# Four small elementwise steps of a gated-attention and GEGLU kernel moved from VectorE to GpSimd

## The chip, the cores and the metric

The kernel runs on one core of a Trainium2 chip. The metric is device time in microseconds (us). Most executions of a kernel agree within some tenths of a per cent. On one core, a run counts as slow when it is over 1.5% above the fastest of the same kernel.

The profile's engines are PE (TensorE, matmuls), PEld (TensorE weight loads), DVE (VectorE), ACT (ScalarE), POOL (GpSimd) and SP (SyncE). L189 means line 189 of the kernel that is being profiled. Kernels with inserted lines have shifted numbers.

## The reference, cut to what matters

The lines of the second part are condensed.

```python
# attention part: q, k, v, a_re, a_im are (4, 8, 768, 48), float32
mag = np.sqrt(a_re * a_re + a_im * a_im)
scale = np.minimum(mag, 0.999) / (mag + 1e-06)           # the clamp
a_re_n, a_im_n = (a_re * scale, a_im * scale)
for t in range(S):                                       # a recurrence over the sequence
    new_re = ar * S_re - ai * S_im
    new_im = ar * S_im + ai * S_re
    kv = np.einsum('bhd,bhe->bhde', k[:, :, t], v[:, :, t])
    S_re, S_im = (new_re + kv, new_im)
    y[:, :, t] = np.einsum('bhd,bhde->bhe', q[:, :, t], S_re)
# ... x = y as (3072, 384) tokens ...
ffn_out = gelu(x @ w_gate) * (x @ w_val) @ w_out         # d_ff = 1536
res_gate = 1.0 / (1.0 + np.exp(-(x @ w_res)))
return x + res_gate * ffn_out                            # the residual add
```

The kernel replaces the recurrence by cumulative sums of log-magnitude and phase over blocks of the sequence. Each of the 12 groups holds 256 positions. The sums are carried from group to group.

## The kernel before

The four steps that move are marked.

```python
    def p1_steps(g):                       # log-magnitude of group g
        ...
        def s3():
            act(out=T["s", g], in_=T["s", g], func=AF.Ln, bias=1.0)
            lm = T["lm", g]
            nc.vector.scalar_tensor_tensor(out=lm, in0=T["s", g], scalar=0.5, in1=lm, op0=OP.mult, op1=OP.add)  # L188
            nc.vector.tensor_scalar(out=lm, in0=lm, scalar1=LNMAX, scalar2=None, op0=OP.min)                    # L189: clamp

    def carry(g):                          # phase carried from the group before
        ...
            nc.vector.tensor_tensor(out=P, in0=T["th", g - 1][:, DM:W], in1=T["th", g][:, 0:DM], op=OP.add)     # L215
            if s > 1:
                nc.vector.tensor_tensor(out=P, in0=P, in1=T["P", g - 1], op=OP.add)                             # L217

    def cs_t(g, c):                        # phase -> fraction of a turn
        ...                                # matmuls L227, L229 (L229 reads P), then L234, L235 on DVE
        if c == C - 1:
            nc.vector.scalar_tensor_tensor(out=fg[:, :, 0, :], in0=fg[:, :, 1, :], ...)                         # L237

    def turn(nm, g, srcs):                 # a row, turned to partitions by way of DRAM
        ...
        for i, src in enumerate(srcs):
            nc.gpsimd.dma_start(out=md[i:i + 1, :], in_=src)                                                    # L253
        for u in range(2):
            nc.gpsimd.dma_start(out=m[u * D:(u + 1) * D]..., in_=md...)                                         # L256: two halves

    def decay3(g):                         # M: the decay of the carried state
        m = T["m2", g]
        M = mp.tile([128, H], FP, tag="M", name="M")
        nc.vector.tensor_tensor(out=M[0:DD], in0=m[0:DD, 0], in1=m[0:DD, 1], op=OP.mult)                        # L273
        nc.vector.tensor_tensor(out=M[0:DD], in0=M[0:DD], in1=T["m1", g][0:DD, 0], op=OP.mult)                  # L274
    ...
    def op_step(u, jj):                    # output projection; ot comes from a pool of two buffers
        ...
        nc.vector.scalar_tensor_tensor(out=ot, in0=T["sg", u][:, jj], scalar=1.0, in1=ps, ...)                  # L437
        nc.vector.tensor_tensor(out=ot, in0=ot, in1=T["x", u * 4 + jj], op=OP.add)                              # L438: residual add
        nc.sync.dma_start(out=out[t0:t0 + 128, :], in_=ot)
```

GpSimd issues the turn transfers, the weight loads and the loads of `v`. M (L273) needs both halves of a turn transfer, and it stands in DVE's program order among the `fg` and `xT` work: in this kernel behind the second `fg` and `xT` of X1 and X2 (M of `m_1264` at 139.79 us, of `m_1910` at 186.16 us).

ScalarE's table loads cut the time into stretches. Pro is the prologue. Y0 to Y4 are the stretches with the gelu table, where the gate and value matmuls run. X1 to X4 are the stretches between them (Ln, Exp, Arctan, Sin). A tail follows.

## Time and profile before

The kernel before took 343.4 us (median of 3 runs, 342.9 to 344.4). The profiled execution spans 341.4 us.

| stretch | length, us | TensorE busy, us | granted clock |
|---|---|---|---|
| Pro (prologue) | 94.0 | 40.6 | 0.75 |
| Y0 | 26.0 | 24.4 | 1.00 |
| X1, Y1 | 20.8, 26.4 | 17.3, 25.7 | 1.00, 1.00 |
| X2, Y2 | 20.1, 26.6 | 16.1, 26.1 | 1.00, 1.00 |
| X3, Y3 | 20.7, 25.6 | 16.2, 25.3 | 1.00, 1.00 |
| X4, Y4 | 18.5, 26.0 | 17.3, 25.7 | 1.00, 1.00 |
| tail | 36.9 | 32.8 | 1.00 |

In the Y stretches the TensorE has hardly any idle time. In the X stretches it has about 13 us in all. So a lighter DVE can only help in X. A rule for reading what follows: work slides across the border of an X and the Y behind it, so such a pair is read as one number.

These are lines of the page of the kernel before: the span; busy time, share of the span and instruction count of four engines; and the activity in 40 equal slices, in tenths (PEclk is the granted TensorE clock).

```profile
span 341.4 us, 5552 instructions
PE 267.3 (78%) x2054; PEld 160.6 (47%) x2080; DVE 245.4 (72%) x440; ACT 203.0 (59%) x338; POOL 67.1 (20%) x104
...
PE   0330544298689979899897999779999989999995
DVE  1322696249999649999389998499994799855443
POOL 9423710050522224102232000150001300000000
PEclk9996585559699999999999999999999999999999
```

DVE is busy 72% of the time and GpSimd 20%, which is what invites the change.

These are the groups of DVE instructions by line and shape. After the bar come the total busy us and the mean ns of one, then the idle time before them.

```profile
L330 DVE TENSOR_TENSOR atm<-at,mask_81 128x512 bf16<-128x512 f32 x48 | 32.8, 683 | 7.2 <-PE at L327 7.2
...
L438 DVE TENSOR_TENSOR ot<-ot,x 128x384 f32<-128x384 f32 x24 | 13.2, 552 | 0.3
...
L237 DVE SCALAR_TENSOR_TENSOR fg<-fg 128x768 f32<-128x768 f32 x12 | 11.4, 949 | 0.0
...
L285 DVE TENSOR_TENSOR kE<-k,Ei 128x768 bf16<-128x768 f32 x12 | 11.4, 947 | 0.0
...
L189 DVE TENSOR_SCALAR ar<-ar 128x768 f32<-128x768 f32 x12 | 6.9, 592 | 0.1
```

The moved steps cost DVE 0.59 us (clamp) and 0.55 us (each add).

This is one line of GpSimd's timeline in X2: start, duration, then the instruction. Both halves of the transfer that M needs are issued back to back.

```profile
177.82 1.51 POOL L256 DMA_DIRECT2D m_1910<-dm_1907  x2 [0.63 <-issue]
```

### The profile page before, as it was taken

Reading aid. Unit: us, or ns where it says so; the run is one execution under the profiler, and the core shown is the slowest. Engines: PE = TensorE matmul, PEld = TensorE weight load, DVE = VectorE, ACT = ScalarE, POOL = GpSimd, SP = SyncE. Lnnn points to the kernel's source line nnn. Section 1 sums busy time; section 2 is a strip of 40 time slices with the busy share of each in tenths; the row PEclk is TensorE's granted clock in tenths of the full one; section 3 lists DMA queues with packets and bytes.
Section 4 is the critical chain, followed back from the end, with each engine's and each line's share of the span. In section 5 each row is a group of like instructions: output and inputs, shape, how many; then the busy total and the mean of one; then the engine's idle time right before and its main releaser. Section 6 shows DMA issues by size and latency. Waiting matters only on the chain.

```text
span 341.4 us, 5552 instructions
## 1 busy us (share of the span) xinstructions
PE 267.3 (78%) x2054; PEld 160.6 (47%) x2080; DVE 245.4 (72%) x440; ACT 203.0 (59%) x338; POOL 67.1 (20%) x104
## 2 busy tenths in 40 slices
PE   0330544298689979899897999779999989999995
PEld 0110224275256545465554566445665556565452
DVE  1322696249999649999389998499994799855443
ACT  3365434349665696756896656977568275662530
POOL 9423710050522224102232000150001300000000
PEclk9996585559699999999999999999999999999999
DMA  9999999999999999527422620021000210002002
GB/s 139 136 139 175 176 184 196 175 170 171 155 167 162 169 133 172 109 46 72 25 63 54 118 46 2 2 48 47 3 2 1 50 46 2 0 2 92 2 1 92
DMA packets 135258, 30.25 MB, mean 89 GB/s; under 512 B 127168, under 2 KB 135232, under 8 KB 135232
## 3 DMA queue, kind: packets, MB, share of 16 engines
q1 hardware_dynamic: 103296, 23.60, 40.6%
q0 software_dynamic: 31936, 6.31, 21.9%
q8 instruction: 16, 0.26, 0.3%
q14 instruction: 10, 0.08, 0.1%
HBM read 31.33 MB, written 4.76 MB: 106 GB/s over the span
## 4 chain that ended last, share of the span: by engine, by line
PE 47%; DMA 18%; DVE 15%; ACT 9%; issue 7%; POOL 3%; ACTq 0%; DVEq 0%; POOLq 0%
PE vp L414 12%; PE gp L410 11%; PE op L434 6%; DMA dm_266<-ar 4%; DMA v<-in_v_dram 4%; PE tp L320 3%; PE at L327 3%; PE tp L317 3%; PE rp L426 3%; DMA dm_663<-Ei 2%; ACT L445 2%; DVE fg L237 2%; DVE r L234 2%; DMA dm_219<-ar 2%; ACT CS L119 2%
## 5 line engine op out<-in xcount | busy, mean ns | idle before, releaser
L410 PE MATMUL gp<-xT,wg 128*128 128x512 bf16 x196 | 61.5, 382 | 7.6 <-DVE xT L401 4.6
L414 PE MATMUL vp<-xT,wv 128*128 128x512 bf16 x210 | 60.3, 382 | 0.3
L322 ACT COPY qk<-tp 96x512 bf16<-96x512 bf16 x48 | 27.9, 581 | 28.3 <-PE tp L320 15.1
L180 DVE TENSOR_TENSOR ai<-s,ai 128x768 f32<-128x768 f32 x12 | 11.1, 955 | 38.5 <-ACT s L119 26.9
L330 DVE TENSOR_TENSOR atm<-at,mask_81 128x512 bf16<-128x512 f32 x48 | 32.8, 683 | 7.2 <-PE at L327 7.2
L410 PEld LDWEIGHTS <-wg 128*128 128x128 bf16 x216 | 20.0, 98 | 23.0 <-issue 8.9
L317 PE MATMUL tp<-ident,Q 128*96 128x128 bf16 x192 | 20.1, 231 | 13.4 <-DVE qk L323 8.6
L142 POOL DMA_DIRECT2D v<-in_v_dram x24 | 21.3, 902 | 43.0 <-PE y L367 22.4
L414 PEld LDWEIGHTS <-wv 128*128 128x128 bf16 x216 | 20.4, 98 | 19.3 <-issue 0.8
L317 PEld LDWEIGHTS <-Q 128*96 128x96 bf16 x192 | 17.3, 131 | 21.4 <-issue 10.0
L323 DVE COPY qk<-tp 96x512 bf16<-96x512 bf16 x48 | 19.9, 414 | 10.1 <-ACT qk L322 9.6
L203 PE MATMUL csl<-ar,lt0a 128*128 128x384 f32 x24 | 12.3, 601 | 18.6 <-DVE ar L189 18.5
L119 ACT ACTIVATE CS<-fg,hpi 128x768 bf16<-128x768 f32 x12 | 11.2, 935 | 24.1 <-DVE fg L237 24.1
L445 ACT ACT_TABLE_LOAD x18 | 23.1, 1283 | 1.0 <-PEq L547 0.7
L320 PE MATMUL tp<-ident,K 128*96 128x128 bf16 x192 | 22.1, 235 | 0.0
L227 PE MATMUL cst<-ai,lt0b 128*128 128x384 f32 x24 | 11.6, 568 | 13.4 <-ACT ai L119 13.1
L327 PE MATMUL at<-qk 96*128 96x128 bf16 x192 | 20.4, 228 | 0.1
L437 DVE SCALAR_TENSOR_TENSOR ot<-sg,op 128x384 f32<-128x384 f32 x24 | 13.2, 549 | 9.4 <-PE op L434 9.4
L365 PE MATMUL y<-v,atm 128*128 128x48 bf16 x192 | 17.9, 187 | 2.5 <-DVE atm L330 2.4
L365 PEld LDWEIGHTS <-atm 128*128 128x128 bf16 x192 | 13.5, 98 | 12.8 <-DVE atm L330 11.6
L320 PEld LDWEIGHTS <-K 128*96 128x96 bf16 x192 | 17.3, 133 | 0.0
L357 PEld LDWEIGHTS <-K 128*96 128x96 bf16 x160 | 13.3, 138 | 6.5 <-DVE K L292 4.2
(155 smaller groups left out, 626.3 us busy)
## 6 DMA issues: line engine op xcount, KB each, us to landing
ar<-in_a_re_dram SPq DMA_DIRECT2D x24, 192.0 KB, 5.7
ai<-in_a_im_dram SPq DMA_DIRECT2D x24, 192.0 KB, 5.5
q<-in_q_dram SPq DMA_DIRECT2D x24, 192.0 KB, 5.1
k<-in_k_dram SPq DMA_DIRECT2D x24, 192.0 KB, 5.0
out_dram<-ot SPq DMA_DIRECT2D x24, 192.0 KB, 1.9
v<-in_v_dram POOLq DMA_DIRECT2D x24, 96.0 KB, 6.3
wg<-in_moe_w_gate_dram POOLq DMA_DIRECT2D x4, 288.0 KB, 9.2
wv<-in_moe_w_val_dram POOLq DMA_DIRECT2D x4, 288.0 KB, 10.5
```

The lines of the kernel that those rows point to most:

```text
L142: nc.gpsimd.dma_start(out=t[:, c], in_=rows(v, g, c))
L317: nc.tensor.transpose(out=tp[0:DD, j * 128:j * 128 + 128], in_=Q(x), identity=ident)
L320: nc.tensor.transpose(out=tp[0:DD, 512 + j * 128:640 + j * 128], in_=K(x), identity=ident)
L322: nc.scalar.copy(out=qk[0:DD, 0:512], in_=tp[0:DD, 0:512])
L323: nc.vector.tensor_copy(out=qk[0:DD, 512:1024], in_=tp[0:DD, 512:1024])
L327: nc.tensor.matmul(out=at[:, j], lhsT=qk[0:DD, 512 + j * 128:640 + j * 128], rhs=qk[0:DD, j * 128:j * 128 + 128], start=True, stop=True)
L330: nc.vector.tensor_tensor(out=atm, in0=at, in1=mask4, op=OP.mult)
L365: nc.tensor.matmul(out=ys, lhsT=st["atm", hg][:, j], rhs=V(h), start=True, stop=first)
L410: nc.tensor.matmul(out=gp, lhsT=wg[:, fi, ffi * 128:(ffi + 1) * 128], rhs=xT[:, fi, :], start=(fi == 0), stop=(fi == KD - 1))
L414: nc.tensor.matmul(out=vp, lhsT=wv[:, fi, ffi * 128:(ffi + 1) * 128], rhs=xT[:, fi, :], start=(fi == 0), stop=(fi == KD - 1))
L434: nc.tensor.matmul(out=ps, lhsT=h2[:, ffi, jj * 128:(jj + 1) * 128], rhs=wo[:, ffi, :], start=(ffi == 0), stop=(ffi == KF - 1))
L445: tab(nc.scalar.preload_act_table_set(nm))
```

## The change

The intent is to unload DVE by giving four steps to the engine that is idle most of the time. Here is the whole diff, with lines of context cut.

```diff
@@ p1_steps, s3
-            nc.vector.tensor_scalar(out=lm, in0=lm, scalar1=LNMAX, scalar2=None, op0=OP.min)
+            nc.gpsimd.tensor_scalar(out=lm, in0=lm, scalar1=LNMAX, scalar2=None, op0=OP.min)
@@ carry
-            nc.vector.tensor_tensor(out=P, in0=T["th", g - 1][:, DM:W], in1=T["th", g][:, 0:DM], op=OP.add)
+            nc.gpsimd.tensor_tensor(out=P, in0=T["th", g - 1][:, DM:W], in1=T["th", g][:, 0:DM], op=OP.add)
             if s > 1:
-                nc.vector.tensor_tensor(out=P, in0=P, in1=T["P", g - 1], op=OP.add)
+                nc.gpsimd.tensor_tensor(out=P, in0=P, in1=T["P", g - 1], op=OP.add)
@@ op_step
-        nc.vector.tensor_tensor(out=ot, in0=ot, in1=T["x", u * 4 + jj], op=OP.add)
+        nc.gpsimd.tensor_tensor(out=ot, in0=ot, in1=T["x", u * 4 + jj], op=OP.add)
```

The diff doesn't show that the scheduler of this framework places the instructions anew, so the order on every engine changes as well. One such move matters: in X1 and X2, M now stands ahead of the second `fg`.

## The prediction

> **What bounds the kernel now.** Three regimes (activity by slices, busy time by windows).
> (1) Up to about 90 us the TensorE is mostly idle. The DMA engines are full (tenths at 9), and the chain of waits runs through small GpSimd-issued turn transfers: 21.8 us dm_219 (6.9 us), 31.3 m_247 (5.6), 44.8 dm_266 (13.9, behind the weight loads in the same queue).
> (2) From 96 us on, phases that run gate/value matmuls are TensorE-bound (23.2 of 24, 24.3 of 25, 25.6 of 26 us busy).
> (3) Between them are phases of about 20 us (120-142, 167-189, 214-233) with TensorE at 18.5 of 22, 17.8 of 22, 14.7 of 19 us. Their chain is ScalarE Ln/Exp, then an unbroken DVE row up to the second fg (L237), then Sin, table load, Gelu. Only here can a lighter DVE pay; 12 us of TensorE idle is the ceiling.
>
> **What moves (groups by line).** DVE loses 12 clamps (0.59 us each), 8+4 carry adds (0.55), 24 residual adds (0.55): 26.5 of 245 us. DVE instructions follow each other about 0.47 us apart, so a middle phase loses two clamps and three residual adds ahead of the second fg: about 2.3 us. GpSimd gains 48 instructions. Estimate, from the Trainium skill, "GPSIMD Engine Reference", section "Performance versus the Vector engine" (about 2.6 cycles per element with two inputs, 1.8 with one): 0.9-1.2 us each, so GpSimd busy rises from 67 to about 115 us. The trace before has no such instruction to check it.
>
> **Critical path.** Clamp and carry are used a phase later, except in the prologue; the residual add only feeds the output, except the last one. By themselves they are off the path. What matters is GpSimd's in-order queue, which also issues the turn DMAs. The instruction order of the changed kernel puts
> - the clamp of group 2 ahead of all weight loads. It waits for L188 (38.0 us before), so weights start about 3.5 us later, and dm_266 lands behind them;
> - clamps and residual adds between the two halves of m_1264 and m_1910. M (L273) stands on DVE ahead of the second fg in those phases, so DVE will wait for their landing: I estimate 3-4 us each (the last half issued at about 136 and 182 us, 3-4 us to land), more than the 2.3 us saved. In the phase at 214-233 us m_2538 is ahead of the residual adds: there the gain of about 2 us stays.
> Also, DVE operations with two SBUF inputs (L180, L188, L237, L280, L285, L292) may block against GpSimd's reads (Trainium skill, "SBUF — State Buffer", section "Who interferes with whom"). The trace before doesn't show it; I allow 0.2-0.4 us per GpSimd instruction, which returns about half of the 26 us.
> Sum: prologue 0 to +3 (the DVE row at 81-95 us loses 1.2), phase 120-142 +2, 167-189 +1, 214-233 -1.5, 259-280 +0.5, tail +0.7 (a slower residual add plus a hop).
>
> **Prediction.** 346.0 us, 8 in 10 between 339.5 and 353.0. Faster by over 2%: 0.04; within 2%: 0.76; slower by over 2%: 0.20.
>
> **Signs.** Right: DVE busy about 222-232 us; GpSimd 105-125; weights issued from about 40 us; DVE waits of some us at M for m_1264 and m_1910; two-input DVE operations with longer means; the last phases' TensorE busy time unchanged. Wrong: no waits at M and gelu starting earlier in every middle phase (then 338-340 us); or GpSimd instructions of 2 us and more (then over 350).
>
> **What would make it wrong.** The whole order was rescheduled: more attention work precedes the stall near 55-64 us, which may hide the later weights. Delayed v loads may let the first a-tiles land sooner. Port blocking may be far heavier than allowed.

## More of the kernel before

L237 and L285 read two operands from SBUF. L330 reads one from SBUF and one from PSUM.

## The result, and the profile after

The changed kernel is correct and slower. It took 356.64 us (median of 4 runs, 354.1 to 360.6; the longest counts as slow, and the three fast ones, up to 357.0, have the median 356.33), and the kernel before took 343.73 us in the same rounds. The ratio is 1.035, 95% interval 1.029 to 1.042. Ratios in this document are the mean time of one kernel's fast runs over that of the other's in the same rounds, so they are not quite the ratio of the medians that stand beside them. The profiled run is a fast one.

The same lines of the page of the changed kernel:

```profile
span 354.6 us, 5635 instructions
PE 274.0 (77%) x2080; PEld 160.7 (45%) x2080; DVE 232.0 (65%) x392; ACT 203.6 (57%) x338; POOL 139.4 (39%) x152
...
PE   0330507795399987799884999898999989999994
DVE  1312666677887477898395997398984699853431
POOL 6673490534942159502159400079500720003013
PEclk9995656588889999899999899999999999999998
```

DVE fell by 13.4 us only. GpSimd gained 72 us, where about 48 were expected. TensorE became busier by 6.7 us with the same matmuls. A few matmul records are missing in the first trace (x2054 against x2080), which may be part of that; the clock row shows another reason: it now dips in several slices.

Groups by line and shape of the changed kernel, DVE then GpSimd:

```profile
L330 DVE TENSOR_TENSOR atm<-at,mask_81 128x512 bf16<-128x512 f32 x48 | 32.9, 686 | 13.6 <-PE at L327 13.6
...
L237 DVE SCALAR_TENSOR_TENSOR fg<-fg 128x768 f32<-128x768 f32 x12 | 13.5, 1125 | 0.1
...
L285 DVE TENSOR_TENSOR kE<-k,Ei 128x768 bf16<-128x768 f32 x12 | 12.8, 1070 | 0.0
```

```profile
L438 POOL TENSOR_TENSOR ot<-ot,x 128x384 f32<-128x384 f32 x24 | 27.6, 1157 | 60.6 <-DVE ot L437 59.5
...
L189 POOL TENSOR_SCALAR ar<-ar 128x768 f32<-128x768 f32 x12 | 28.1, 2344 | 15.4 <-DVE ar L188 15.2
```

A clamp takes 2.34 us on GpSimd (at best 2.12) where DVE took 0.59. An add takes 1.16 us (at best 0.90) where DVE took 0.55. DVE's operations with two SBUF inputs became longer (L237 from 949 to 1125 ns). L330, with one input in PSUM, did not (683 and 686). Over all DVE groups that both kernels have, the lengthening adds up to 7.9 us (the sum over groups of the difference of means times the count).

GpSimd's timeline of the changed kernel in X2. The clamp now stands between the two halves of the transfer:

```profile
183.70 2.12 POOL L189 TENSOR_SCALAR ar<-ar 128x768 f32<-128x768 f32 x1 [0.84 <-DVE ar L188]
185.81 0.91 POOL L438 TENSOR_TENSOR ot<-ot,x 128x384 f32<-128x384 f32 x1
186.67 0.83 POOL L256 DMA_DIRECT2D m_1910<-dm_1907  x1
187.54 2.83 POOL L189 TENSOR_SCALAR ar<-ar 128x768 f32<-128x768 f32 x1
190.34 0.79 POOL L256 DMA_DIRECT2D m_1910<-dm_1907  x1
```

DVE's timeline of the changed kernel at the same place. The bracket is the idle time before an instruction, and what ended it:

```profile
188.31 0.54 DVE L234 TENSOR_SCALAR r<-cst 128x384 f32<-128x384 f32 x1
193.10 0.66 DVE L273 TENSOR_TENSOR M<-m_1910 96x8 f32<-96x8 f32 x1 [4.25 <-DMA m_1910<-dm_1907]
```

DVE does nothing for 4.25 us, in front of the second `fg`, `xT` and Q. In X1 it waits 2.25 us for `m_1264` in the same way. Two things meet here: the transfer is later, and M stands ahead of the second `fg` (which runs at 194.62 us) and no longer behind it.

On the TensorE this becomes a gap, as the waits of TensorE before and after show (what it waited for: us in total, times, longest). The 2.1 us of the kernel before lie in the prologue; ahead of Y1 and Y2 it waited 0.97 and 0.78 us there:

```profile
PE gp L410 <- DVE xT L401: 4.6, 4, 2.1
```

```profile
PE gp L410 <- DVE xT L401: 10.1, 4, 4.9
```

The gap costs more than its own length. The next fence has the changed kernel at the end of X1, by stretches of 1 us. The columns are the length, then busy us (and count) of PE, PEld, DVE, ACT and POOL, then the granted clock, the DMA share and GB/s.

```profile
141.00:142.00 1.00, 0.00 (x0) 0.00 (x0) 1.00 (x2) 0.00 (x0) 0.67 (x1) 1.00 1.32 185
142.00:143.00 1.00, 0.00 (x0) 0.00 (x0) 1.00 (x3) 0.00 (x0) 0.00 (x0) 1.00 1.44 200
143.00:144.00 1.00, 0.18 (x1) 0.10 (x1) 1.00 (x5) 0.46 (x1) 0.00 (x0) 1.00 0.48 58
144.00:145.00 1.00, 1.00 (x5) 0.37 (x4) 1.00 (x2) 1.00 (x2) 0.84 (x2) 0.69 0.02 2
145.00:146.00 1.00, 1.00 (x7) 0.75 (x6) 1.00 (x4) 0.98 (x2) 0.99 (x2) 0.50 0.13 1
146.00:147.00 1.00, 1.00 (x4) 0.30 (x2) 1.00 (x2) 0.99 (x2) 1.00 (x1) 0.50 0.18 18
147.00:148.00 1.00, 1.00 (x4) 0.40 (x3) 1.00 (x2) 0.34 (x2) 1.00 (x1) 0.60 0.00 0
```

After 3.42 us without a matmul the clock is granted at half for about 3.4 us. Over these four stretches that takes 0.31 + 0.50 + 0.50 + 0.40 = 1.7 us of full-speed matmul time. The Trainium skill, "TensorE: Matmul & The Clock Gate", section "Part 1: The HAM clock gate", states this behaviour: an idle window of about 3.4 us sets the array to half rate, and about as long a busy window releases it. Gaps of 3.42 and 4.9 us are each followed by 0.50 for about 3.4 us. But no length of gap is shown above which the clock falls. A gap of 2.50 us in X2/Y2 of e4 (below) left it at 1.00, while in e6 it fell to 0.50 at 239.67 us with no gap of over 1.33 us in the stretch before. That stretch of e6, in the same columns, shows TensorE busy for 1.44 of 3.41 us:

```profile
236.26:239.67 3.41, 1.44 (x18) 0.95 (x19) 3.41 (x4) 1.46 (x2) 3.33 (x5) 1.00 0.02 2
```

Lengths of the pairs in the profiled executions, with some of the experiments that follow:

| kernel | Pro+Y0 | X1+Y1 | X2+Y2 | X3+Y3 | X4+Y4 | tail | span |
|---|---|---|---|---|---|---|---|
| before | 120.0 | 47.2 | 46.7 | 46.2 | 44.5 | 36.9 | 341.4 |
| after | 121.8 | 51.0 | 52.1 | 47.3 | 44.6 | 37.9 | 354.6 |
| e6: after, M moved | 120.8 | 47.9 | 47.0 | 50.5 | 44.3 | 37.6 | 348.0 |
| e7: before, M moved | 119.4 | 46.9 | 46.5 | 46.3 | 43.2 | 36.9 | 339.1 |
| e10: e7, residual add on GpSimd | 118.2 | 49.3 | 48.3 | 49.2 | 44.3 | 38.0 | 347.3 |
| e13: e7, GpSimd repeats all four | 118.1 | 52.6 | 50.8 | 51.6 | 44.4 | 38.3 | 355.7 |
| e14: e7, GpSimd only writes | 117.1 | 53.5 | 48.2 | 48.6 | 43.2 | 38.3 | 348.9 |
| e15: e7 again | 116.5 | 46.9 | 46.5 | 46.2 | 43.2 | 36.9 | 336.2 |

Pro+Y0 differs by 2.9 us between e7 and e15, which are the same kernel, while all their other pairs agree within 0.1 us. So differences of less than 3 us in the first column are not read. Of the change's 13.2 us, 3.9 + 5.4 = 9.3 us are in the pairs 1 and 2, the two in which DVE waits at M.

### The profile page after: what moved, and what is told of

Read it like the earlier page. It is cut to its first block, busy times and chain, and to the rows that moved or that the text cites. A ratio compares the mean times of both kernels' runs of the same rounds, so it can differ in the third digit from the quotient of the medians.

```text
span 354.6 us, 5635 instructions
## 1 busy us (share of the span) xinstructions
PE 274.0 (77%) x2080; PEld 160.7 (45%) x2080; DVE 232.0 (65%) x392; ACT 203.6 (57%) x338; POOL 139.4 (39%) x152
## 4 chain that ended last, share of the span: by engine, by line
PE 52%; SPq 15%; DMA 10%; DVE 8%; ACT 6%; issue 4%; POOL 4%; POOLq 0%; ACTq 0%; DVEq 0%
PE gp L410 13%; PE vp L414 13%; SPq L131 9%; PE op L434 7%; SPq L138 7%; PE rp L426 3%; DMA k<-in_k_dram 3%; DMA dm_663<-Ei 3%; PE tp L317 3%; PE tp L320 3%; PE at L327 3%; PE cst L227 2%; PE y L365 2%; PE dk L357 1%; ACT L445 1%
## 5 line engine op out<-in xcount | busy, mean ns | idle before, releaser
L410 PE MATMUL gp<-xT,wg 128*128 128x512 bf16 x216 | 66.8, 393 | 11.3 <-DVE xT L401 10.1
L414 PE MATMUL vp<-xT,wv 128*128 128x512 bf16 x216 | 64.9, 392 | 0.5 <-ACT h_2670 L119 0.5
L438 POOL TENSOR_TENSOR ot<-ot,x 128x384 f32<-128x384 f32 x24 | 27.6, 1157 | 60.6 <-DVE ot L437 59.5
L322 ACT COPY qk<-tp 96x512 bf16<-96x512 bf16 x48 | 27.9, 581 | 36.8 <-PE dk L357 16.4
L330 DVE TENSOR_TENSOR atm<-at,mask_81 128x512 bf16<-128x512 f32 x48 | 32.9, 686 | 13.6 <-PE at L327 13.6
L189 POOL TENSOR_SCALAR ar<-ar 128x768 f32<-128x768 f32 x12 | 28.1, 2344 | 15.4 <-DVE ar L188 15.2
L445 ACT ACT_TABLE_LOAD x18 | 23.1, 1283 | 1.0 <-PEq L547 0.7
L323 DVE COPY qk<-tp 96x512 bf16<-96x512 bf16 x48 | 19.8, 412 | 2.2 <-ACT qk L322 2.0
L365 PEld LDWEIGHTS <-atm 128*128 128x128 bf16 x192 | 12.9, 98 | 15.3 <-DVE atm L330 14.8
L327 PE MATMUL at<-qk 96*128 96x128 bf16 x192 | 19.5, 224 | 0.0
```

What stands on the lines that cost most here:

```text
L189: nc.gpsimd.tensor_scalar(out=lm, in0=lm, scalar1=LNMAX, scalar2=None, op0=OP.min)
L322: nc.scalar.copy(out=qk[0:DD, 0:512], in_=tp[0:DD, 0:512])
L327: nc.tensor.matmul(out=at[:, j], lhsT=qk[0:DD, 512 + j * 128:640 + j * 128], rhs=qk[0:DD, j * 128:j * 128 + 128], start=True, stop=True)
L330: nc.vector.tensor_tensor(out=atm, in0=at, in1=mask4, op=OP.mult)
L365: nc.tensor.matmul(out=ys, lhsT=st["atm", hg][:, j], rhs=V(h), start=True, stop=first)
L410: nc.tensor.matmul(out=gp, lhsT=wg[:, fi, ffi * 128:(ffi + 1) * 128], rhs=xT[:, fi, :], start=(fi == 0), stop=(fi == KD - 1))
```

## The experiments

Two theories were set against each other. The "queue" theory says that GpSimd's in-order instruction stream is longer, so what it issues or finishes comes later, and DVE stands waiting for it. The "port" theory says that GpSimd and DVE share SBUF access, so DVE's instructions get longer. Later the first was split into the part at M, the half clock that follows, and the rest. Because M can be moved, it became possible to test them apart.

### One step at a time (e1, e2, e3)

The edits are the first, the second and the third part of the diff above, each alone on the kernel before.

> Only the 12 clamps go to GpSimd; carry adds and residual adds stay on DVE. Queue theory (the loss comes from GpSimd's in-order queue: turn transfers stand behind the new instructions, and DVE waits at M, L273): here only the phase near 167-189 us has M ahead of the second fg, so one wait of about 2 us at M for m_1910, weights issued about 5 us later than before: total 345 to 349 us. Port theory (DVE is slowed by GpSimd's reads): clamps are the longest instructions (2.1 us each, 28 of the 68 us added), so about half of the loss, 349 to 351 us, with no wait at M over 1 us.

> Only the 8+4 carry adds go to GpSimd. M stands on DVE where it stood before, after the second fg. Queue theory: within 1.5 us of before, 343 to 345 us. Port theory: 12 of the 68 us added on GpSimd, so about a sixth of the loss, 345 to 346 us.

> Only the 24 residual adds go to GpSimd. M for m_1264 and m_1910 stands after the second fg, only M for m_1258 ahead of it. Queue theory: no wait of over 1 us at M ahead of the second fg, DVE row in the middle phases shorter by about 1.4 us each, tail about 0.8 us longer: 340 to 345 us. Port theory: 28 of the 68 us added on GpSimd, so about 40% of the loss: 347 to 350 us.

The kernel before took 344.2 us in these rounds. The results:
- e1 (clamp): 346.03 us, ratio 1.0045 (0.9988 to 1.0101).
- e2 (carry): 350.58 us, ratio 1.0175 (1.0121 to 1.0228).
- e3 (residual): 348.09 us, ratio 1.0111 (1.0063 to 1.0159).

None of the four steps helps, not even alone. e1's time lies in the queue theory's range, but not for its reason: there is no wait at M in X1 or X2, although M of `m_1910` stands ahead of the second `fg` there too. e3's time is in the port theory's range, with no wait at M in X1 or X2. e2 was a miss for both theories. Its profile shows the TensorE matmul of L229 waiting 3.5 us for P, and 2.5 us for K. The adds had been put into the GpSimd stream behind the loads of the output weights (2.27 us of issuing) and of `v`. That wait is in the prologue (at 74 us). Outside it, X3 is 1.4 us longer, and there a residual add on DVE took 1.89 instead of 0.55 us beside two carry adds on GpSimd.

### M later in the changed kernel (e4)

M is pinned behind the second `fg` and the `xT` copy in DVE's order. GpSimd's order is unchanged.

```diff
+        i = nc.vector.tensor_tensor(out=M[0:DD], in0=m[0:DD, 0], in1=m[0:DD, 1], op=OP.mult)
+        for late in ("fgl", "xtl"):      # the last fg (L237) and the last xT copy
+            if late in T:
+                tc.add_manual_dep(i.ins, T[late].ins.name, order, reason="M late")
```

> The changed kernel, with an ordering edge that places M (L273) on DVE after the second fg and the xT copy. GpSimd's order is word for word that of the changed kernel, so its port load is the same. Queue theory: the waits of 2.2 and 4.2 us at M ahead of the second fg go, and with them 1 us each of the following phase in which TensorE had started late: 347 to 351 us. Port theory: nothing changes but those waits move, 354 to 357 us.

Measured: 350.08 us (349.3 to 351.5), ratio 1.0174 (1.0134 to 1.0213). About half of the loss came back. So with the transfers as late as in the changed kernel, M's new place was needed for that half; and by e1, that place without the late transfer costs no wait. X1 and X2 fell to 20.0 and 19.8 us. But Y2 grew to 30.1 us: M still stood in front of Q there and waited 2.0 us, and the TensorE waited 2.5 us for Q. (Y0 grew to 30.2 us, but the prologue fell; the two together are 121.5 us, within the spread.)

### M behind Q and K (e6, e7, e8)

M is moved behind the K product of its group, in the changed kernel (e6) and, as a control, in the kernel before (e7).

```diff
-                nc.vector.tensor_tensor(out=t, in0=T["CS", g], in1=sb, op=OP.mult)
+                T["last"] = nc.vector.tensor_tensor(out=t, in0=T["CS", g], in1=sb, op=OP.mult)
 ...    # decay3
+        tc.add_manual_dep(i.ins, T["last"].ins.name, order, reason="M after K")
 ...    # phase_x: dec3 taken out;  phase_y:
-        pr = [st for g in gs(u + 1) for st in products(g)]
+        pr = [st for g in gs(u + 1) for st in products(g) + ([call(decay3, g)] if g % NS > 0 else [])]
```

> The changed kernel with M (L273, the two small products of the turned row maxima) moved behind the K product on DVE, so that neither the second fg nor Q, xT nor K stands behind its waits for the turn DMAs. Theory 'M': the loss of 12.6 us is M's waits on DVE, which delay xT, open gaps on TensorE and lower the granted clock of the gate/value phases. Then X1 and X2 come to about 20-21 us each (23.5 and 24.5 in the changed kernel), the clock of Y0 to Y4 is 0.99-1.00, and the time is 338-344 us. Theory 'port': DVE's two-input operations are stretched by 48 GpSimd instructions of 1-2.3 us, whatever waits on M. Then the stretched means stay (L237 1125 ns, L285 1070) under both, but the time stays at 350 us or more.

> Control: the same move of M in the kernel before. Both theories: 340-345 us, X1 20-21, X2 19.5-20.5. The difference between this run and e6 is what the four steps on GpSimd cost or save once M is out of the way: theory 'M' expects e6 to be within 3 us of this run, theory 'port' expects e6 to be 7 us or more slower.

The kernel before took 343.97 us in these rounds. The results:
- e6: 349.52 us (349.2 to 351.0), ratio 1.0177 (1.0130 to 1.0225).
- e7: 339.83 us (338.6 to 342.1), ratio 0.9894 (0.9829 to 0.9959).

Pairs 1 and 2 fell from 51.0 and 52.1 to 47.9 and 47.0 us, within 0.8 us of the kernel before. The clock of Y1 and Y2 rose from 0.95 and 0.97 to 1.00. So M's wait was the cause of the loss in these two pairs: 3.2 + 5.1 = 8.3 of the 9.3 us.

But the theory that M explains the whole was wrong. It expected e6 within 3 us of e7, and the difference is 9.7 us, as the port theory expected. The lengthening of DVE's groups rose from 7.9 us in the changed kernel to 15.3 us in e6. In e4, whose order on GpSimd is that of the changed kernel, it was already 14.5 us. The reading is that DVE could not be held up in any other way while it stood at M, so removing the wait exposed the other cost. Part of it is in Y3 (29.7 us, clock 0.94). There DVE waited 1.17 us for an output buffer and its K product took 1.75 us. The TensorE waited for Q and K, and the clock fell to 0.50 for three stretches of 1 us.

> e6 with four output buffers (ot) instead of two, so that DVE's first output step need not wait for the store that now follows a GpSimd add. In the changed kernel that wait ended 1.2 us of DVE idle time (phase at about 240 us). Expected under both theories: 0 to 1.5 us less than e6; no change if that wait is off the path.

The edit is `bufs=2` to `bufs=4` for the pool of `ot`. e8's three fast runs took 343.9, 346.7 and 347.0 us, ratio 1.0063 (0.9992 to 1.0134); the fourth, 351.4 us, is slow. The order on DVE, GpSimd, TensorE and ScalarE is that of e6. So the output buffers account for about 3 to 4 us (the intervals of the two ratios just touch), more than the 0 to 1.5 us expected. Its profile fell in the slow run, so no times are read from it.

### TensorE's gap filled (e9)

Twelve unread 128x512 matmuls follow the last output projection in X1 and X2 of the changed kernel. The Q transposes are pinned behind them.

```diff
+    def warm():
+        with tc.high_priority():
+            sc = psM.tile([128, 512], FP, tag="mm", name="warm")
+            for _ in range(12):
+                i = nc.tensor.matmul(out=sc, lhsT=wg[:, 0, 0:128], rhs=wg[:, 0, 0:512], start=True, stop=True)
```

> The changed kernel with 12 unread 128x512 matmuls put into TensorE's gap before the gate/value phases Y1 and Y2 (about 2.6 us of work in gaps of 3.4 and 4.9 us), with M's waits left as they are. Theory 'clock': the gap lowers the granted clock of the phase behind it (Y1 0.95, Y2 0.97). Then Y1 and Y2 come to 0.99-1.00 and shorten by 1.2 and 0.8 us (27.6 to 26.4, 27.6 to 26.8), and the time falls by 1-3 us. Rival, the phases are longer because of DVE (stretched operations) and the clock dips on its own: Y1 and Y2 stay at 27.6 and 0.95-0.97, time unchanged or longer by up to 2 us. The scheduler moves some attention work behind the unread matmuls, so the phase lengths count more than the total.

Measured: 362.19 us (360.8 to 363.9), ratio 1.055. The clock theory was right about the clock of Y1 and wrong about the time. These are stretches of 1 us of e9 behind the filled gap, in the columns used before:

```profile
144.00:145.00 1.00, 1.00 (x9) 0.40 (x6) 1.00 (x3) 0.98 (x3) 1.00 (x2) 1.00 0.00 0
145.00:146.00 1.00, 0.21 (x1) 0.00 (x0) 1.00 (x3) 1.00 (x1) 0.99 (x2) 1.00 0.16 2
146.00:147.00 1.00, 0.36 (x7) 0.37 (x8) 1.00 (x2) 0.23 (x1) 1.00 (x1) 1.00 0.09 1
```

The clock of Y1 is 1.00 instead of 0.95 and Y1's TensorE busy time is 26.8 instead of 27.6 us. The filler left gaps of 1.83 and 1.43 us in place of one of 3.42 us. So here it is the idle time that lowers the clock. Yet Y1 is longer (28.5 us): the TensorE now waits 1.43 us for K, and real work was pushed behind the unread matmuls. In X2 the filler came too late. A gap of 3.26 us stayed, the clock fell to 0.50 for 3.4 us as before, and Y2 is 29.5 instead of 27.6 us, so for Y2 the expectation failed. The half clock makes a gap dearer, but its origin is on DVE.

### Each step with M out of the way (e10, e11, e12)

The base is e7. The edits are the three parts of the diff again, one at a time.

> The kernel before with M moved behind the K product (339.8 us alone), and of the change only the 24 residual adds on GpSimd. The three single steps are to show whether any of the four is worth having once M no longer waits on DVE in the middle phases. Theory 'offload pays once the queue wait is gone': 336-339 us, each middle phase X1 to X4 shorter by up to 1 us. Theory 'contention': the adds (0.9-1.2 us each) block DVE's two-input operations and the wait for an output buffer (1.2 us) appears: 341-345 us.

> As e10, with only the 12 clamps on GpSimd. Theory 'offload pays once the queue wait is gone': 337-340 us. Theory 'contention': a clamp holds GpSimd and the shared reads for 2.1 us and stretches L237, L280 and L285 beside it: 340-344 us, with the prologue 2-3 us longer as in e1 (97.0 instead of 94.0 us).

> As e10, with only the 12 carry adds on GpSimd. In e2 these were the worst of the three (346.4 us span): TensorE's cst matmul waited 3.5 us for P, because the adds stood behind v's DMAs in the GpSimd queue. Both theories: 342-347 us, with a wait of 2 us or more of TensorE for P at L217 again.

The kernel before took 344.3 us in these rounds. The base e7 has a ratio of 0.989. The results:
- e10 (residual): 348.72 us, ratio 1.014 (1.0073 to 1.0206).
- e11 (clamp): 340.59 us, ratio 0.9885 (0.983 to 0.9941).
- e12 (carry): 344.23 us, ratio 0.997 (0.9901 to 1.0039), with the same 3.5 us wait for P.

The clamp, the slowest of the four on GpSimd, costs nothing. The residual add, which DVE does in 0.55 us, costs about 8.5 us over 24 instances. e10's expectation (341 to 345 us under contention) was too low. Two places of X2 in e10 show one part of the reason, on DVE and then on GpSimd at the same times:

```profile
179.15 2.19 DVE L188 SCALAR_TENSOR_TENSOR ar<-s,ar 128x768 f32<-128x768 f32 x1
...
186.12 1.83 DVE L237 SCALAR_TENSOR_TENSOR fg<-fg 128x768 f32<-128x768 f32 x1
```

```profile
179.59 0.92 POOL L439 TENSOR_TENSOR ot<-ot,x 128x384 f32<-128x384 f32 x1
...
186.20 0.92 POOL L439 TENSOR_TENSOR ot<-ot,x 128x384 f32<-128x384 f32 x1
```

L237 takes 0.95 us when alone. Beside an add of 0.92 us it takes 1.83, nearly the sum. The DVE row up to the second `fg` is the critical one in X, and the residual adds fall into it. Half a microsecond taken off DVE comes back as up to 0.9 us. L188 at 179.15 was held up longer than the add lasted (2.19 us), with a DMA issue of GpSimd on either side of the add; which of them held it is open. In X3 of e10 DVE also stood 1.78 us in front of an output step (at 234.88 us); the profile names no releaser. Four output buffers, as in e8, were not tried on e10.

### GpSimd works twice, DVE keeps everything (e13)

All four steps stay on DVE, on the base e7. GpSimd does each of the 48 operations again, into a tile that nobody reads. The order of instructions on DVE and TensorE is word for word that of e7.

```diff
             nc.vector.tensor_scalar(out=lm, in0=lm, scalar1=LNMAX, scalar2=None, op0=OP.min)
+            nc.gpsimd.tensor_scalar(out=ghost, in0=lm, scalar1=LNMAX, scalar2=None, op0=OP.min)
 ...    # likewise behind the adds L215, L217 and L438
+        nc.gpsimd.tensor_tensor(out=ghost[:, 0:DM], in0=ot, in1=T["x", u * 4 + jj], op=OP.add)
```

> The kernel before with M moved, all four steps kept on DVE, and GpSimd doing each of the 48 operations a second time into a tile that nobody reads. The order of instructions on DVE and TensorE is word for word that of e7; nothing waits for GpSimd's results. So it measures contention and the lengthened GpSimd queue alone. Theory 'contention and queue': DVE's two-input operations from SBUF are longer by 5 us or more in sum, and the time is 345-352 us, most of the way from e7 (339.8) to e6 (349.5). Theory 'slower results': what costs is that csl, cst, P and the output wait for a slower engine; then e13 stays at 339-342 us.

Measured: 357.92 us (356.2 to 358.4), ratio 1.038 (1.0322 to 1.0439). DVE's busy time rises from 245.9 to 263.3 us with no instruction added to it. Nobody waits for a result of GpSimd here, except that an `ot` buffer is held until GpSimd has read it too (DVE waited 2.8 us for that). So the theory that consumers wait for slower results is not needed for a loss of this size (the changed kernel does have one such wait, 4.8 us for P, in the prologue). Work beside DVE is costly in itself, even more than expected (345 to 352 us).

### The same, but GpSimd only writes (e14)

The 48 pieces now read one element and then only write, with memsets of about the same total length. DVE's and TensorE's order is again that of e7.

```diff
+    def hold(src, *widths):
+        nc.gpsimd.tensor_copy(out=ghost[0:1, 0:1], in_=src[0:1, 0:1])
+        for n in widths:
+            nc.gpsimd.memset(ghost[:, 0:n], 0.0)
 ...    # hold(lm, 768, 768, 384) behind the clamp, hold(..., 768) behind each add
```

> As e13 (M moved, all four steps on DVE, 48 unread pieces of GpSimd work behind the same DVE results), but the pieces only write: a copy of one element, then memsets of 768 elements, one in place of an add and two and a half in place of a clamp. Estimated from this case's memsets (205 ns for 128 elements, 98 ns for one) they hold GpSimd about as long, 1.0 and 2.2 us. The order on DVE and TensorE is that of e7 and e13. Theory 'shared reads': what costs in e13 is that GpSimd reads SBUF while DVE reads two operands. Then DVE's busy time falls from 263 us (e13) to 245-249 us and the time from 357.9 to 340-345 us. Theory 'queue': what costs is that GpSimd is occupied, so that the turn, weight and v transfers are issued later. Then the time stays at 352 us or more though DVE's operations are short.

Measured: 350.72 us (348.6 to 351.7), ratio 1.0166 (1.0111 to 1.0221), between what the two theories expected. Groups by line and shape of e13 and then of e14, for the same four operations (L189, L290, L241 and L190 in e13 are L195, L296, L247 and L196 in e14):

```profile
L189 DVE SCALAR_TENSOR_TENSOR ar<-s,ar 128x768 f32<-128x768 f32 x12 | 15.2, 1283 | 2.8 <-ACT s L120 2.8
...
L290 DVE TENSOR_TENSOR kE<-k,Ei 128x768 bf16<-128x768 f32 x12 | 12.8, 1068 | 0.0
...
L241 DVE SCALAR_TENSOR_TENSOR fg<-fg 128x768 f32<-128x768 f32 x12 | 12.7, 1061 | 0.1
...
L190 DVE TENSOR_SCALAR ar<-ar 128x768 f32<-128x768 f32 x12 | 8.3, 713 | 0.1
```

```profile
L195 DVE SCALAR_TENSOR_TENSOR ar<-s,ar 128x768 f32<-128x768 f32 x12 | 11.2, 952 | 2.8 <-ACT s L126 2.8
...
L296 DVE TENSOR_TENSOR kE<-k,Ei 128x768 bf16<-128x768 f32 x12 | 11.4, 947 | 0.0
...
L247 DVE SCALAR_TENSOR_TENSOR fg<-fg 128x768 f32<-128x768 f32 x12 | 11.4, 949 | 0.1
...
L196 DVE TENSOR_SCALAR ar<-ar 128x768 f32<-128x768 f32 x12 | 9.5, 809 | 0.1
```

Without GpSimd's reads the operations with two SBUF inputs are back at the 947 to 953 ns that they have in e7. The lengthening over all groups is 16.3 us in e13 and 1.8 us in e14. So it is GpSimd's reads that lengthen them, which the Trainium skill, "SBUF — State Buffer", section "Who interferes with whom", states: a DVE instruction with two SBUF inputs contends with a GpSimd instruction that reads SBUF, not with one that only writes. The operation with one input and a float32 output (the clamp, 596 ns in e7) is longer beside pure writes, too: 809 ns. The same section names the two-port modes of such operations as contending; no run here shows in which mode the clamp ran.

Going from e13 to e14 gives back 7.2 us. The other 9 to 11 us, from e7's 339.8 or e15's 341.4 (below) to 350.7, are the occupied queue. Nearly 7 us of it is in one pair, X1+Y1. There DVE stood before an output step, because the buffer's last reader was waiting its turn on GpSimd. This is DVE's timeline of e14:

```profile
140.62 0.56 DVE L448 SCALAR_TENSOR_TENSOR ot<-sg,op 128x384 f32<-128x384 f32 x1 [3.72 <-POOL ghost L81]
```

The clock fell again behind this wait: Y1 is 32.2 us long at a clock of 0.89. e13 has no such wait at this place, and its pair 1 is shorter (52.6 against 53.5 us). In the pairs 2 and 3, e13 is 9.6 us longer than e7 and e14 4.1 us, so there the reads are more than half. e14 is not a perfect copy of e13's queue, since some of its pieces lie between other DMA issues. So the split of about 7 us for reads and 10 us for the queue is this pair's, not a law.

### The best version again (e15)

> The same kernel as e7 again, in five rounds, for a tighter interval: it was 1.1% faster than the kernel before in three rounds, 95% interval 0.983 to 0.996. Expected from e7: a ratio of 0.985 to 0.993, 339-341 us. If the gain was chance: a ratio of 0.995 or more.

Measured: 341.37 us (338.0 to 342.5, 6 runs) beside 344.86, ratio 0.9896 (0.9851 to 0.9941). The kernel before with M moved behind K, and all four steps on DVE, is 1% faster than the kernel before. That is less than the 2% that would count as faster, but the interval excludes 1. It beats both kernels.

Apart from the prologue, e7's gain in the profile is in X4+Y4: 44.5 to 43.2 us. The kernel before had waited 1.8 us at M for `m_3118` there.

## Why the prediction was wrong

The prediction was 346.0 us (339.5 to 353.0), within 2% as the likeliest outcome. It is 356.64 us and 3.5% slower. In the prediction's own terms, the step that failed is its sum over the stretches: it put X1 and X2 at +2 and +1 us and has no term for the Y stretches. Measured are 9.3 us in the pairs 1 and 2. The waits at M that it named were right, but not what they cost behind them.

- **Right: the queue at M.** "DVE will wait for their landing: I estimate 3-4 us each." It waited 2.25 us for `m_1264` and 4.25 us for `m_1910`, neither within 3 to 4 but right in sum. e6 showed that this is 8.3 us of the loss in the profile. That X3 has no such wait was also right (X3 -1.0 us; -1.5 predicted).
- **The term that was missing: the stretches behind.** The sum has terms for the prologue, the four X stretches and the tail, and the signs say "the last phases' TensorE busy time unchanged". Y0 to Y4 grew by 1.6, 1.2, 1.0, 2.0 and 1.5 us, together 7.4 of the 13.2 us. In Y3 and Y4 most of that is work that slid over from X. In Y1 and Y2 it was the half clock after gaps of 3.42 and 4.9 us, a cost that a sum of waits does not contain: at mean clocks of 0.95 and 0.97 it is 1.4 and 0.8 us of 27.6 us. The trace before already showed gaps of 0.97 and 0.78 us before `gp` at these places, to which the waits at M were to be added.
- **Mis-sized: X2.** Predicted +1 us, measured +4.4. The prediction set a wait of 3-4 us against 2.3 us saved on DVE. The wait was 4.25 us, and little was saved: the second `fg` could only start after M.
- **Mis-sized: GpSimd's instructions.** The estimate of 0.9 to 1.2 us each was taken from the Trainium skill, "GPSIMD Engine Reference", section "Performance versus the Vector engine". For the two-input adds it holds (at best 0.90 us). For the one-input clamp it does not: 2.12 us at best, 2.34 on average. The page gives the 1.8 cycles as a best case of a tight loop; taking it for the clamp was the prediction's own step. So GpSimd was busy 139 us, not 105 to 125, and a clamp between two halves of a transfer delayed the second by 2.8 us. The prediction named "GpSimd instructions of 2 us and more (then over 350)" as a sign against it, and that is what came. But slow clamps by themselves are not what costs: on e7, with M out of their way, they cost nothing (e11).
- **Port blocking: near in size, wrong in weight.** It was allowed 0.2-0.4 us per instruction. The lengthening was 7.9 us over 48 instructions, 0.16 us each. DVE's busy time, 232.0 us, is at the edge of the predicted 222 to 232. Not foreseen was that DVE's waits at M hid some of it (15.3 us once they were gone), and that the residual adds, "by themselves off the path", hit the DVE row that is on it (e10: +2.5 points of ratio against e7).
- **Weights 3.5 us later**: they were issued at 43.1 instead of 36.8 us, 6.3 us later. Pro+Y0 grew by 1.8 us, which is within the spread of one kernel.

What stays open: how the cost of the four steps adds up exactly (alone on the kernel before they cost 1.8, 6.4 and 3.9 us, and on e7 about 0, 3 and 8.5), what held L188 for 2.19 us, how much of the residual add's cost is the wait for output buffers, and how much of e14's queue cost the changed kernel itself has.

## What to carry to other kernels

A step that is off the critical path may still be costly on GpSimd. Here it delayed the transfers that GpSimd issued behind it (by 2.8 us for one half), and its SBUF reads held up DVE's two-input operations: one add that saved DVE 0.55 us took back 0.88 us. Before moving work to an idle engine, look for what else that engine feeds, and first move any small instruction that waits for it (here M) out of the busy engine's way; that alone gave 1%. Where TensorE already idles ahead of a dense stretch (0.97 and 0.78 us here), an added wait can end in a half clock of 3.4 us, and the next stretch pays again. After a reschedule, look also at where the waiting instruction now stands.

## What the Trainium skill lacked or had wrong

- "GPSIMD Engine Reference", section "4.1 Engine selection", calls one-input elementwise work on GpSimd "roughly line-rate", and the section "Performance versus the Vector engine" gives a best case of about 1.8 cycles per element. The clamp of 128x768 float32 took 2.12 us at best, against 0.59 us on DVE and about 1.15 us estimated from that figure. The two-input add agreed (0.90 us for 384 elements, and about 0.83 estimated from 2.6 cycles per element at 1.2 GHz).
- "SBUF — State Buffer", section "Who interferes with whom", agrees on reads and on writes (1061 to 1283 ns with reads beside them, 947 to 952 with writes only). It does not say what remains of a saving: DVE gave up 26.9 us of instructions (the sum of their durations), 7.9 us came back as longer ones, and its busy time, in which overlapping instructions count once, fell by 13.4 us.
- "TensorE: Matmul & The Clock Gate", "Part 1: The HAM clock gate", agrees (0.50 for about 3.4 us after a gap of 3.42 us). It gives no share of busy time below which a stretch counts as idle: in e6 TensorE was busy for 1.44 of the 3.41 us before the half clock. It does not say that filling the gap with unread matmuls can lose more than it wins: in e9 the clock of Y1 was 1.00, and Y1 was longer than without (28.5 and 27.6 us).
- In none of the pages that were read: elementwise work on GpSimd delays the transfers that it issues. Two halves that had been issued in 1.51 us together were 3.67 us apart (186.67 and 190.34 us), which, with M's new place, became a DVE wait of 4.25 us.
